# Costs of GpSimd's work in a list scheduler: wide operations in parts of 128 columns, four chunks converted early instead of five, four PSUM banks for y instead of five

## The chip, the cores and the metric

The kernel runs on one core of a Trainium2 chip. The metric is device time in microseconds of the whole program. Three runs of the kernel before took 821.39, 822.38 and 822.40 us (median 822.38 us). PE is the matrix engine TensorE, DVE is VectorE, ACT is ScalarE, POOL is GpSimd, SP issues the DMAs.

## What is computed

Three blocks follow each other, all in fp32:

```python
a = exp(phi - max(phi, axis=2)); a = a / (sum(a, axis=2) + 1e-9)
k_m, v_m = einsum('bhsm,bhsd->bhmd', a, k), einsum('bhsm,bhsd->bhmd', a, v)   # 32 memory slots
attn = softmax(q @ k_m^T / 8);  x = attn @ v_m          # 4 batches, 8 heads, 576 positions, 64 wide
h = x @ w_in;  g = maximum(0.01 * h, h);  x = g @ w_out                # 2304 x 512, inner width 2048
y = ((x @ w_a) * (x @ w_b)) @ w_out2                                   # inner width 1536
```

## The kernel before

Each fp32 product is made as three products of parts: a tensor is split into a high part (a rounded copy) and a low part (the tensor less its high part), and the products high*high, high*low and low*high are added in PSUM. So each operand needs a copy and a subtraction on ACT, DVE or POOL. The weights are first brought to another bit form: for each 512 KB tile of weights ACT makes two passes, and then `clamp` (L455), `shift` (L459), `join` (L463) and `add` (L466) follow, then the copy `hi` and the subtraction `lo` (L472). `shift` and `join` are DVE's alone; `clamp`, `add` and `lo` may go to DVE or to POOL.

The first MLP goes through four chunks c of 512 inner columns and, in each, eight tiles n of 288 tokens: four units h (24 matmuls in all), each followed by two passes of ACT and a subtraction g (L789, on DVE or POOL), and four units y (48 matmuls), each of which DVE adds into an accumulator (L815). Before the tiles of a chunk stand the products vw (L724), whose results ACT and DVE take from PSUM. The second MLP goes through twelve chunks of 128 columns, twice: for half s=0 and half s=1 of the tokens. Each chunk needs a tile of w_a, of w_b and of w_out2, and sums of w_a and w_b (`ws`, L954) with their splits (`wo`, L971). The first PRE chunks (5 before) are converted beside the first MLP and kept in HBM; the others are converted in half s=0 when they come, and kept too; half s=1 reads all of them back. PSUM's eight banks b0 to b7 are given to kinds of tiles by the table ROOMS: h has b0 to b2, y of the first chunk b3 and b4, y of the later chunks (`yx`) b3 to b7, vw and the other small products (`x`) b5 to b7.

The order of every engine's work is set by a list scheduler in the kernel itself (class `Program`) when the program is built. It knows a cost for each operation on each engine that may do it, gives each operation a latest time from its consumers, and goes forward in time: the free engine takes the most urgent ready operation, if no other engine would finish it sooner (`POOL_BIAS` of 0.8 us is counted against POOL) and a buffer is free. Operations of class `Port` on DVE and POOL exclude each other in its plan. It repeats this up to six times and keeps the shortest plan. On the chip each engine then works through its own list in order, and waits for semaphores where data or buffers come later than planned. The conversions are in these lists among the additions and subtractions that PE waits for.

The names that matter below: `c_pool2` (L69, POOL's cost of an operation with n columns), `two` (L362, an operation for DVE or POOL), `weight` (L429) with its costs, `y_unit` (L793, which takes its bank from `yx` from the second chunk on), `w_sums`, and PRE.

Of the kernel before, what the change touches and what calls it, by code (L numbers as in the profile page):

```python
# [66 lines left out]


def c_pool2(n):  # L69
    return 0.25 + n * 2.15e-3  # L70


def c_dve2(n):
# [14 lines left out]
class Op:  # L90
# [3 lines left out]
class Program:  # L94
# [58 lines left out]
    def order(self, target):  # L153
# [25 lines left out]
        ends, times, done, now, got = [], [0.0, 1.7], [], 0.0, {}  # L179
# [33 lines left out]
        main = sorted((o for o in self.ops if o.pos is not None), key=lambda o: o.pos)  # L213
        index = {o.seq: i for i, o in enumerate(main)}
        nth = 0
        while left:
# [59 lines left out]
            if times:  # L276
                nxt = min(nxt, times[0])
            if nxt > 5000:
                raise RuntimeError(f"no room: at {now} main {main[nth:nth+1] and main[nth].tiles} held {sorted(map(str,(k for k,t in held.items() if t[0]!='b')))}  ready {[(e, [x.tiles for x in r][:4]) for e, r in ready.items() if r]}")
            now = nxt  # L280
            while ends and ends[0][0] <= now + 1e-9:
                o = self.ops[heappop(ends)[1]]
# [6 lines left out]
    def run(self, make, rounds=6):  # L289
        main = [o for o in self.ops if o.pos is not None]  # L290
        main.sort(key=lambda o: o.pos)
        target, t = {}, START
        for o in main:
            target[o.seq] = t
            t += o.cost
        best, self.tries = None, []
        for _ in range(rounds):
            self.urgency(target)
            done, got = self.order(target)
            end = max(o.end for o in done)  # L300
# [23 lines left out]
def tile_mem_attention__leaky_mlp__bilinear_mlp(  # L324
# [20 lines left out]
    nc = tc.nc  # L345
# [8 lines left out]
    op, tile_of = pr.op, pr.tile  # L354
# [2 lines left out]
        pool = ps if tag[0] == "b" else sb  # L357
        return pool.tile([parts, *shape], dtype, tag=tag, name="_".join(map(str, key)))

    engines = {"DVE": nc.vector, "POOL": nc.gpsimd}  # L360

    def two(n):  # L362

# [30 lines left out]
    def zeros(T):  # L394
# [34 lines left out]
    def weight(kind, c, k, after=()):  # L429
# [44 lines left out]
        a = ("a", key)  # L474
# [1 line left out]
        op("DMA", c_dma(524288), load, r=after, w=[raw], tiles=[raw], ahead=1e12 if early else 30.0, keep=8 if early else 2 if late else 7 if c < 2 else 4)  # L476
        op("ACT", 0.66, high, r=[raw], w=[a], tiles=[raw, cv], ahead=1e12 if early else 25.0, keep=6 if early else 0 if late else 5 if c < 2 else 2)
        op("ACT", 0.66, low, r=[raw], w=[("l", key)], tiles=[raw, cv], ahead=any_time)
        op(Port({"DVE": 0.42, "POOL": 2.0}), 0, clamp, w=[a], tiles=[cv], ahead=any_time)
        op(Port({"DVE": 0.42}), 0, shift, w=[a], tiles=[cv], ahead=any_time)  # L480
        op(Port({"DVE": 0.68}), 0, join, r=[raw], w=[a], tiles=[raw, cv], ahead=any_time)
        op(Port({"DVE": 0.62, "POOL": 1.35}), 0, add, r=[("l", key)], w=[a], tiles=[cv], ahead=any_time)
        if kind in ("wa", "wb"):
            return
        if kind == "wout2" and by_seven(1, c):
# [866 lines left out]
```

## Time and profile before

| | |
|---|---|
| median of three runs | 822.38 us |
| profiled execution, whole | 821.03 us |
| its span, first to last instruction | 819.3 us |
| PE, DVE, ACT, POOL busy | 785.8, 681.0, 374.6, 239.2 us |
| PE's waits, longest in total | for ACT's first exponential 6.0 us, for DVE's kvn 4.1, for DVE's g 3.9, for DVE's accumulator 3.2 |
| first MLP / second MLP, about | 50 to 410 us / 410 to 819 us |

A busy PE is one that has matmuls in flight; with no wait 112 matmuls of 512 columns start in 25 us. What a wait on PE costs is read from stretches in which PE's busy time is under the stretch's length, and from the granted clock. What makes PE wait is read from the list of waits and from the rows of the engine named there, in order of time: the length of one instruction against the length that its form has when nothing is beside it.

### The profile page before, as it was taken

How to read it: one execution, taken by the hardware profiler on the slowest of the kernel's cores; microseconds unless marked ns; L12 is line 12 of the kernel's file. 1: busy time of each engine (PE TensorE's matmuls, PEld its weight loads, DVE VectorE, ACT ScalarE, POOL GpSimd, SP SyncE). 2: the span in 40 equal slices, each digit the busy share in tenths (PEclk: the TensorE clock that was granted, in tenths of full speed). 3: DMA queues.
4: the chain of work that ended last, by engine and by line, in shares of the span. 5: the costliest groups of instructions: out<-in, count | busy, mean ns of one | idle time of the engine just before them, and what ended most of it. 6: DMA issues, size and time to landing. Idle time of an engine off the chain costs nothing.

```text
span 819.3 us, 13254 instructions
## 1 busy us (share of the span) xinstructions
PE 785.8 (96%) x4898; PEld 700.9 (86%) x4898; DVE 681.0 (83%) x1225; ACT 374.6 (46%) x811; POOL 239.2 (29%) x223
## 2 busy tenths in 40 slices
PE   5789999999889999999999999999999999999998
PEld 4568899999889998999988888888888888887886
DVE  6998898689978999899674889999975686898875
ACT  5656776776546664665232534343411153122010
POOL 5562446124601352155000023332300131254300
PEclk8899999999989999999999999999999999999999
DMA  9885301074224530424797565574579788655402
GB/s 331 312 276 174 130 1 53 27 254 152 73 88 172 206 124 27 168 78 180 270 335 281 167 240 198 205 239 173 208 282 330 266 270 284 232 187 194 161 1 102
DMA packets 55936, 152.64 MB, mean 186 GB/s; under 512 B 6976, under 2 KB 20288, under 8 KB 55872
## 3 DMA queue, kind: packets, MB, share of 16 engines
q1 hardware_dynamic: 55872, 151.80, 53.4%
q8 instruction: 38, 0.62, 0.3%
q14 instruction: 26, 0.21, 0.1%
HBM read 106.17 MB, written 45.61 MB: 185 GB/s over the span
## 4 chain that ended last, share of the span: by engine, by line
PE 76%; DVE 14%; DMA 5%; issue 3%; ACT 1%; POOL 0%; SPq 0%; DVEq 0%; ACTq 0%
PE y L803 16%; PE o L1099 13%; PE aby L1016 11%; PE h L773 8%; PE abx L1016 7%; PE abz L1016 7%; PE os L1215 4%; DVE g L789 3%; PE b L1067 2%; PE a L1067 2%; PE vw L724 2%; DMA raw_wout<-in_w_out_dram 1%; DVE acc L815 1%; DVE cv_win L463 1%; DVE cv_win L455 1%
## 5 line engine op out<-in xcount | busy, mean ns | idle before, releaser
L803 PE MATMUL y<-g,wout 128*128 128x288 f32 x1536 | 224.1, 299 | 5.2 <-DVE g L789 3.9
L803 PEld LDWEIGHTS y<-g,wout 128*128 128x128 f32 x1536 | 212.8, 191 | 9.6 <-DVE g L789 4.6
L1016 PE MATMUL aby<-yb_T,wo 128*128 128x512 f32 x432 | 110.1, 390 | 0.8 <-DVE t L1024 0.8
L1016 PEld LDWEIGHTS aby<-yb_T,wo 128*128 128x128 f32 x432 | 80.1, 188 | 17.2 <-DVE t L1024 1.2
L1099 PE MATMUL o<-p,wout 128*128 128x512 f32 x384 | 94.2, 390 | 0.0
L1024 DVE TENSOR_TENSOR t<-aby,t 128x512 f32<-128x512 f32 x72 | 49.4, 686 | 48.3 <-PE aby L1016 46.4
L1099 PEld LDWEIGHTS o<-p,wout 128*128 128x128 f32 x384 | 71.9, 188 | 15.4 <-DVE osum L1112 0.3
L773 PE MATMUL h<-ahi,vwh 128*128 128x288 f32 x256 | 76.5, 299 | 1.2 <-ACT ahi L371 1.2
L773 PE MATMUL h<-alo,vwh 128*128 128x288 f32 x256 | 75.9, 297 | 0.8 <-POOL alo L672 0.8
L773 PE MATMUL h<-ahi,vwl 128*128 128x288 f32 x256 | 75.7, 296 | 0.0
L1016 PE MATMUL abx<-yb_B,wo 128*128 128x512 f32 x288 | 73.5, 391 | 0.4 <-ACT t L1027 0.4
L750 ACT ACTIVATE g<-h 128x288 fp32r<-128x288 f32 x128 | 52.5, 410 | 43.5 <-PE h L773 40.3
L789 DVE TENSOR_TENSOR g<-t,g 128x288 fp32r<-128x288 f32 x100 | 60.7, 611 | 5.8 <-ACT t L750 5.5
L1016 PEld LDWEIGHTS abx<-yb_B,wo 128*128 128x128 f32 x288 | 53.2, 188 | 11.3 <-ACT t L1027 0.8
L815 DVE TENSOR_TENSOR acc<-y,acc 128x288 f32<-128x288 f32 x96 | 43.0, 451 | 12.9 <-PE y L803 12.2
L750 ACT ACTIVATE t<-h 128x288 f32<-128x288 f32 x128 | 52.3, 408 | 0.0
L773 PEld LDWEIGHTS h<-ahi,vwh 128*128 128x128 f32 x256 | 48.2, 188 | 3.9 <-issue 2.4
L773 PEld LDWEIGHTS h<-alo,vwh 128*128 128x128 f32 x256 | 48.3, 189 | 1.3 <-POOL alo L672 1.2
L773 PEld LDWEIGHTS h<-ahi,vwl 128*128 128x128 f32 x256 | 48.3, 189 | 0.0
L739 DVE TENSOR_TENSOR vwl<-vw,vwh 64x512 fp32r<-64x512 f32 (+1 forms) x64 | 39.8, 621 | 7.0 <-ACT vwh L371 5.5
L371 ACT CAST p<-t 128x512 fp32r<-128x512 f32 x29 | 18.0, 619 | 55.8 <-DVE t L1045 29.0
L371 ACT CAST vwh<-vw 64x512 fp32r<-64x512 f32 (+2 forms) x61 | 30.6, 504 | 24.2 <-PE vw L724 17.5
(367 smaller groups left out, 1503.9 us busy)
## 6 DMA issues: line engine op xcount, KB each, us to landing
k_wo<-wo SPq DMA_DIRECT2D x28, 512.0 KB, 4.0
wo<-k_wo SPq DMA_DIRECT2D x28, 512.0 KB, 4.2
raw_wout<-in_w_out_dram SPq DMA_DIRECT2D x23, 512.0 KB, 5.4
raw_win<-in_w_in_dram SPq DMA_DIRECT2D x16, 512.0 KB, 6.4
kv<-in_kv_dram SPq DMA_DIRECT2D x16, 512.0 KB, 9.2
k_yb_T<-yb_T SPq DMA_DIRECT2D x8, 512.0 KB, 6.4
yb_T<-k_yb_T SPq DMA_DIRECT2D x8, 512.0 KB, 5.0
raw_wa<-in_w_a_dram SPq DMA_DIRECT2D x7, 512.0 KB, 4.6
```

The source lines that it names most:

```text
L371: nc.scalar.copy(dst, src)
L739: nc.vector.tensor_tensor(T[lk][to, j // 2, cols], T[o][i * 64:(i + 1) * 64, :], T[hk][to, j // 2, cols].bitcast(F32), op=ALU.subtract)
L750: nc.scalar.activation(dst, src, AF.Prelu, alpha=0.01)
L773: nc.tensor.matmul(T[o], T[w[u]][:, k, fs], T[a[v]][:, k, cols], start=(k == 0 and i == 0), stop=(k == 1 and i == 2))
L789: lambda T, e: engines[e].tensor_tensor(T[g][:, i, 1, :], T[t], T[g][:, i, 0, :].bitcast(F32), op=ALU.subtract),
L803: nc.tensor.matmul(T[o], w[:, u, es], g[:, v, :], start=(f == 0 and i == 0), stop=(f == 3 and i == 2))
L815: "DVE", c_dve(NB), lambda T: nc.vector.tensor_tensor(T[acc][:, e, :], T[o], T[acc][:, e, :], op=ALU.add),
L1016: nc.tensor.matmul(T[o], T[w][:, which, u, k * P:(k + 1) * P], T[ys[v]][:, k, :], start=first and k == 0 and x == 0, stop=k == 1 and x == ...
L1024: op("DVE", 0.69, lambda T: nc.vector.tensor_tensor(T[to], T[o], T[x], op=ALU.add), r=[o, x], w=[to], tiles=[o, x, to])
L1067: nc.tensor.matmul(T[o], T[w][:, k // 2, u, k % 2 * P:(k % 2 + 1) * P], T[ys[v]][:, k, :], start=(k == 0 and x == 0), stop=(k == 3 and x = ...
L1099: nc.tensor.matmul(T[o], T[w][:, u, es], T[g][:, at, v, :], start=(x == 0 and k == 0), stop=(x == 1 and k == 2))
L1215: nc.tensor.matmul(T[o], lhs(T, u), T[g][:, v, :], start=k == 0, stop=k == 2)
```

## The change

POOL's costs in the scheduler are new, and the operations of 448 columns or more that POOL gets are issued as four instructions of 128 columns each (or 64 times 2). PRE is 4, and `yx` has four banks, so that b7 is left to `x`. If a round of the scheduler finds no room, the best plan so far is taken.

```diff
-    "yx": ["b3", "b4", "b5", "b6", "b7"],
+    "yx": ["b3", "b4", "b5", "b6"],
...
-PRE = 5
+PRE = 4
...
 def c_pool2(n):
-    return 0.25 + n * 2.15e-3
+    return 0.45 + n * 1.5e-3 if n < 448 else n * 4.8e-3
...
+            try:
+                done, got = self.order(target)
+            except NoRoom:
+                if best is None:
+                    raise
+                break
...
-    engines = {"DVE": nc.vector, "POOL": nc.gpsimd}
+    class InParts:
+        @staticmethod
+        def cuts(ap):
...
+            if size < 448:
+                return [(slice(None),)]
+            m = size // shape[-1]
+            k = max(1, 128 // m) if shape[-1] * m > 128 else shape[-1]
+            return [(slice(None),) * len(shape) + (slice(i, min(shape[-1], i + k)),) for i in range(0, shape[-1], k)]
+
+        def tensor_tensor(self, dst, a, b, op):
+            for x in self.cuts(dst):
+                nc.gpsimd.tensor_tensor(dst[x], a[x], b[x], op=op)
...
+    engines = {"DVE": nc.vector, "POOL": InParts()}
...
-        op(Port({"DVE": 0.42, "POOL": 2.0}), 0, clamp, w=[a], tiles=[cv], ahead=any_time)
+        op(Port({"DVE": 0.42, "POOL": 2.45}), 0, clamp, w=[a], tiles=[cv], ahead=any_time)
...
-        op(Port({"DVE": 0.62, "POOL": 1.35}), 0, add, r=[("l", key)], w=[a], tiles=[cv], ahead=any_time)
+        op(Port({"DVE": 0.62, "POOL": 2.45}), 0, add, r=[("l", key)], w=[a], tiles=[cv], ahead=any_time)
```

A price of 2.45 us in place of 1.35 us moves work from POOL's list to DVE's: POOL has 100 operations of 448 columns or more before and 51 after (in parts), DVE 1225 instructions before and 1273 after. PE's instructions are the same ones, in a slightly other order. SP issues five reads of kept tiles fewer, in half s=0, and as many loads and writes as before. Three places in the lists follow. Names carry the chunk, the tile and a running number; `x4` is four instructions that follow each other.

POOL in the first chunk of the first MLP, from the first two subtractions alo to the last g of tile 0, before:

```order
L672 TENSOR_TENSOR alo_0_418<-at_0_1_0_408,ahi_0_411 128x288
L466 TENSOR_TENSOR cv_wout_0_0_306<-cv_wout_0_0_306 128x512
L789 TENSOR_TENSOR g_0_0_0_451<-t_0_0_0_457,g_0_0_0_451 128x288
L472 TENSOR_TENSOR wout_0_0_461<-cv_wout_0_0_306,wout_0_0_461 128x512
L472 TENSOR_TENSOR wout_0_1_504<-cv_wout_0_1_330,wout_0_1_504 128x512
L789 TENSOR_TENSOR g_0_0_0_451<-t_0_0_1_478,g_0_0_0_451 128x288
L472 TENSOR_TENSOR wout_0_3_540<-cv_wout_0_3_393,wout_0_3_540 128x512
L789 TENSOR_TENSOR g_0_0_1_509<-t_0_0_2_512,g_0_0_1_509 128x288
L789 TENSOR_TENSOR g_0_0_1_509<-t_0_0_3_573,g_0_0_1_509 128x288
```

and with the change:

```order
L387 TENSOR_TENSOR alo_0_424<-at_0_1_0_414,ahi_0_417 128x288
L387 TENSOR_TENSOR g_0_0_0_456<-t_0_0_0_462,g_0_0_0_456 128x288
L387 TENSOR_TENSOR g_0_0_0_456<-t_0_0_1_472,g_0_0_0_456 128x288
L387 TENSOR_TENSOR wout_0_0_483<-cv_wout_0_0_309,wout_0_0_483 128x128 x4
L387 TENSOR_TENSOR g_0_0_1_510<-t_0_0_2_518,g_0_0_1_510 128x288
L387 TENSOR_TENSOR wout_0_3_550<-cv_wout_0_3_399,wout_0_3_550 128x128 x4
L387 TENSOR_TENSOR g_0_0_1_510<-t_0_0_3_577,g_0_0_1_510 128x288
```

The add of wout_0_0 and the subtraction of wout_0_1 have gone to DVE, where the add stands ahead of the instructions kvn that PE waits for and the subtraction behind them; the two g of the first pair come ahead of the wide work.

POOL in the second chunk of the first MLP (c=1), from tile n=3 to the last of the wide operations before the third chunk, before:

```order
L472 TENSOR_TENSOR wout2_0_-1_2625<-cv_wout2_0_-1_2197,wout2_0_-1_2625 128x512
L472 TENSOR_TENSOR win_2_0_2642<-cv_win_2_0_2465,win_2_0_2642 128x512
L466 TENSOR_TENSOR cv_wb_1_-1_2480<-cv_wb_1_-1_2480 128x512
L466 TENSOR_TENSOR cv_wout_2_0_2756<-cv_wout_2_0_2756 128x512
L954 TENSOR_TENSOR ws_1_2859<-cv_wb_1_-1_2480 128x256
L954 TENSOR_TENSOR ws_1_2859<-cv_wa_1_-1_2414,cv_wb_1_-1_2480 128x256
L954 TENSOR_TENSOR ws_1_2859<-ws_1_2859,cv_wa_1_-1_2414 128x256
L472 TENSOR_TENSOR wout_2_0_2886<-cv_wout_2_0_2756,wout_2_0_2886 128x512
L466 TENSOR_TENSOR cv_wout_2_2_2824<-cv_wout_2_2_2824 128x512
L954 TENSOR_TENSOR ws_1_2859<-cv_wa_1_-1_2414,ws_1_2859 128x256
L971 TENSOR_TENSOR wo_-1_1_2_2913<-ws_1_2859,wo_-1_1_2_2913 128x2x256
L971 TENSOR_TENSOR wo_-1_1_1_2895<-cv_wb_1_-1_2480,wo_-1_1_1_2895 128x2x256
```

and with the change:

```order
L391 TENSOR_SCALAR cv_wb_1_-1_2516<-cv_wb_1_-1_2516 128x128 x4
L387 TENSOR_TENSOR wout2_0_-1_2643<-cv_wout2_0_-1_2233,wout2_0_-1_2643 128x128 x4
L387 TENSOR_TENSOR cv_wa_1_-1_2450<-cv_wa_1_-1_2450 128x128 x4
L387 TENSOR_TENSOR g_1_7_1_3011<-t_1_7_3_3047,g_1_7_1_3011 128x288
L387 TENSOR_TENSOR wout_2_3_3042<-cv_wout_2_3_2921,wout_2_3_3042 128x128 x4
L387 TENSOR_TENSOR ws_1_3195<-cv_wa_1_-1_2450,ws_1_3195 128x256
```

Twelve operations have become six, and chunk 1 of the second MLP is converted later: its sums and splits, which stood here, come in the third chunk. From tile n=3 to the first tiles of the third chunk DVE has 105 instructions before and 103 with the change.

POOL in half s=0 of the second MLP, chunks 8 to 10, before:

```order
L971 TENSOR_TENSOR wo_0_9_0_6555<-cv_wa_9_0_6414,wo_0_9_0_6555 128x2x256
L954 TENSOR_TENSOR ws_9_6603<-cv_wa_9_0_6414,cv_wb_9_0_6435 128x256
L971 TENSOR_TENSOR wo_0_9_1_6611<-cv_wb_9_0_6435,wo_0_9_1_6611 128x2x256
L954 TENSOR_TENSOR ws_9_6603<-ws_9_6603,cv_wa_9_0_6414 128x256
L954 TENSOR_TENSOR ws_9_6603<-cv_wa_9_0_6414,ws_9_6603 128x256
L971 TENSOR_TENSOR wo_0_9_2_6665<-ws_9_6603,wo_0_9_2_6665 128x2x256
L971 TENSOR_TENSOR wo_0_9_3_6675<-ws_9_6603,wo_0_9_3_6675 128x2x256
L466 TENSOR_TENSOR cv_wa_10_0_6646<-cv_wa_10_0_6646 128x512
L971 TENSOR_TENSOR wo_0_10_0_6827<-cv_wa_10_0_6646,wo_0_10_0_6827 128x2x256
L455 TENSOR_SCALAR cv_wb_11_0_6837<-cv_wb_11_0_6837 128x512
L466 TENSOR_TENSOR cv_wb_11_0_6837<-cv_wb_11_0_6837 128x512
```

and with the change:

```order
L391 TENSOR_SCALAR cv_wa_10_0_6721<-cv_wa_10_0_6721 128x128 x4
L391 TENSOR_SCALAR cv_wb_10_0_6746<-cv_wb_10_0_6746 128x128 x4
L387 TENSOR_TENSOR ws_9_6821<-cv_wb_9_0_6511 128x256
L387 TENSOR_TENSOR ws_9_6821<-cv_wa_9_0_6487,cv_wb_9_0_6511 128x256
L387 TENSOR_TENSOR ws_9_6821<-cv_wa_9_0_6487,ws_9_6821 128x256
L387 TENSOR_TENSOR wo_0_9_1_6811<-cv_wb_9_0_6511,wo_0_9_1_6811 128x2x64 x4
L387 TENSOR_TENSOR p_0_8_0_6905<-t1_0_8_6724,p_0_8_0_6905 128x128 x4
L391 TENSOR_SCALAR cv_wa_11_0_6918<-cv_wa_11_0_6918 128x128 x4
L391 TENSOR_SCALAR cv_wb_11_0_6951<-cv_wb_11_0_6951 128x128 x4
L391 TENSOR_SCALAR cv_wout2_10_0_6998<-cv_wout2_10_0_6998 128x128 x4
L391 TENSOR_SCALAR cv_wout2_11_0_7020<-cv_wout2_11_0_7020 128x128 x4
```

POOL's splits have gone to DVE and DVE's clamps have come to POOL. In chunks 8 to 10 DVE has 93 instructions before and 99 with the change; POOL has 8 wide and 4 narrow operations before, 11 wide (9 of them clamps) and 5 narrow ones with the change.

## Rows read from the trace of the kernel before

**Rows 1.** The page's first part: busy time of the engines, share of the span, instructions.

```profile
PE 785.8 (96%) x4898; PEld 700.9 (86%) x4898; DVE 681.0 (83%) x1225; ACT 374.6 (46%) x811; POOL 239.2 (29%) x223
```

**Rows 2.** Busy time of each engine in stretches: start and end in us, length, then PE, PEld, DVE, ACT, POOL with their instructions, granted clock of PE, DMA share, GB/s.

```profile
25.00:50.00 25.00, 17.46 (x152) 12.21 (x151) 23.69 (x51) 14.88 (x40) 15.48 (x19) 0.84 0.86 284
...
200.00:225.00 25.00, 23.07 (x170) 22.37 (x168) 25.00 (x41) 14.91 (x35) 13.20 (x11) 1.00 0.29 103
225.00:250.00 25.00, 21.98 (x136) 21.08 (x137) 19.37 (x37) 12.66 (x30) 2.25 (x2) 0.86 0.39 129
...
274.00:315.00 41.00, 39.43 (x294) 39.12 (x294) 40.84 (x71) 23.23 (x55) 17.34 (x12) 1.00 0.30 99
...
423.00:457.00 34.00, 34.00 (x174) 29.09 (x173) 14.87 (x26) 10.85 (x20) 0.00 (x0) 1.00 0.80 291
...
553.00:612.00 59.00, 59.00 (x306) 50.72 (x306) 53.32 (x93) 20.60 (x37) 12.91 (x11) 1.00 0.60 218
612.00:629.00 17.00, 17.00 (x98) 14.96 (x98) 8.82 (x16) 2.50 (x5) 0.00 (x0) 1.00 0.97 348
...
750.00:775.00 25.00, 23.69 (x105) 19.31 (x104) 23.50 (x36) 3.37 (x6) 11.23 (x6) 1.00 0.54 182
```

**Rows 3.** The same view, stretches of the second chunk of the first MLP and what follows.

```profile
184.00:228.00 44.00, 39.25 (x287) 38.08 (x285) 44.00 (x70) 25.24 (x58) 23.30 (x18) 1.00 0.33 117
...
228.00:232.00 4.00, 3.26 (x12) 2.73 (x11) 3.81 (x8) 2.48 (x5) 0.00 (x0) 0.53 0.32 131
232.00:236.00 4.00, 4.00 (x21) 3.96 (x20) 2.51 (x5) 1.00 (x2) 1.92 (x1) 0.62 0.00 0
```

**Rows 4.** PE's waits: who waited, for whom, us in total, times, longest.

```profile
PE kvt L570 <- DVE kvn L562: 4.1, 2, 3.9
PE y L803 <- DVE g L789: 3.9, 3, 1.8
PE vw L724 <- DVE acc L815: 3.2, 2, 2.4
...
PE os L1215 <- DVE osum L1240: 1.3, 1, 1.3
...
PE y L803 <- ACT acc L371: 0.9, 1, 0.9
```

**Rows 5.** DVE in order of time from 217 us: start, length, engine, line, operation, tiles, count.

```profile
217.35 1.42 DVE L789 TENSOR_TENSOR g<-t,g 128x288 fp32r<-128x288 f32 x1
218.70 1.22 DVE L463 SCALAR_TENSOR_TENSOR cv_wout<-raw_wout,cv_wout 128x512 int32<-128x512 int32 x1
219.83 0.45 DVE L815 TENSOR_TENSOR acc<-y,acc 128x288 f32<-128x288 f32 x1
220.20 3.12 DVE L466 CUSTOM_DVE_ANT_0 cv_wout<-cv_wout 128x1024 uint16<-128x1024 uint16 x2
223.25 0.45 DVE L789 TENSOR_TENSOR g<-t,g 128x288 fp32r<-128x288 f32 x1
```

**Rows 6.** POOL in the same stretch.

```profile
217.20 1.26 POOL L466 TENSOR_TENSOR cv_wout<-cv_wout 128x512 int32<-128x512 int32 x1 [1.99 <-issue]
218.42 0.94 POOL L954 TENSOR_TENSOR ws<-cv_wa_-1_2414,ws 128x256 f32<-128x256 f32 x1
219.33 1.74 POOL L971 TENSOR_TENSOR wo_-1_1_2_2913<-ws,wo_-1_1_2_2913 128x512 fp32r<-128x512 f32 x1
221.03 1.74 POOL L971 TENSOR_TENSOR wo_-1_1_1_2895<-cv_wb_-1_2480,wo_-1_1_1_2895 128x512 fp32r<-128x512 f32 x1
```

**Rows 7.** Groups of DVE's instructions by line and shape: count, busy us, mean ns of one, idle before.

```profile
L463 DVE SCALAR_TENSOR_TENSOR cv_wa<-raw_wa,cv_wa 128x512 int32<-128x512 int32 x7 | 4.8, 684 | 0.0
L466 DVE CUSTOM_DVE_ANT_0 cv_wb<-cv_wb 128x1024 uint16<-128x1024 uint16 x6 | 4.1, 685 | 0.1
```

**Rows 8.** Groups of POOL's instructions by line and shape, the same columns.

```profile
L455 POOL TENSOR_SCALAR cv_wout<-cv_wout 128x512 f32<-128x512 f32 x4 | 8.4, 2103 | 3.2 <-ACT cv_wout L448 3.1
L971 POOL TENSOR_TENSOR wo<-cv_wb,wo 128x512 fp32r<-128x512 f32 x6 | 7.8, 1293 | 3.1 <-ACT wo L371 3.1
...
L789 POOL TENSOR_TENSOR g<-t,g 128x288 fp32r<-128x288 f32 x28 | 25.2, 904 | 42.7 <-ACT t L750 31.2 <-PE h L773 11.3
...
L954 POOL TENSOR_TENSOR ws<-cv_wb 128x256 f32<-128x256 f32 x2 | 1.5, 740 | 6.3 <-PE aby L1016 6.2
```

**Rows 9.** DVE and POOL in order of time at three other places: DVE's subtractions with an operand in PSUM beside two wide operations of POOL, and DVE's alo beside a clamp on POOL.

```profile
142.89 4.22 DVE L739 TENSOR_TENSOR vwl<-vw,vwh 64x512 fp32r<-64x512 f32 x6 [0.52 <-ACT vwh L371]
...
144.36 2.54 POOL L472 TENSOR_TENSOR wout<-cv_wout,wout 128x512 fp32r<-128x512 f32 x2 [0.72 <-ACT wout L371]
...
119.47 0.88 DVE L672 TENSOR_TENSOR alo<-at,ahi 128x288 fp32r<-128x288 f32 x2
...
118.56 1.98 POOL L455 TENSOR_SCALAR cv_wout<-cv_wout 128x512 f32<-128x512 f32 x1
```

**Rows 10.** DVE ahead of PE's longest wait for it in the first 50 us, in order of time.

```profile
34.02 4.16 DVE L463 SCALAR_TENSOR_TENSOR cv_wout<-raw_wout,cv_wout 128x512 int32<-128x512 int32 x4
38.11 1.76 DVE L466 CUSTOM_DVE_ANT_0 cv_wout<-cv_wout 128x1024 uint16<-128x1024 uint16 x1
...
40.56 2.34 DVE L466 CUSTOM_DVE_ANT_0 cv_wout<-cv_wout 128x1024 uint16<-128x1024 uint16 x2
...
44.05 2.13 DVE L656 TENSOR_TENSOR sm<-sm,mx 128x288 f32<-128x288 f32 x2
```

More of the change, by code (lines that the diff above doesn't have):

```diff
@@ L85 @@
 class Port(dict):
+    pass
+class NoRoom(RuntimeError):
     pass
@@ L278, in order @@
             if nxt > 5000:
-                raise RuntimeError(f"no room: at {now} main {main[nth:nth+1] and main[nth].tiles} held {sorted(map(str,(k for k,t in held.items() if t[0]!='b')))}  ready {[(e, [x.tiles for x in r][:4]) for e, r in ready.items() if r]}")
+                raise NoRoom(f"no room: at {now} main {main[nth:nth+1] and main[nth].tiles} held {sorted(map(str,(k for k,t in held.items() if t[0]!='b')))}  ready {[(e, [x.tiles for x in r][:4]) for e, r in ready.items() if r]}")
             now = nxt
@@ L298, in run @@
             self.urgency(target)
-            done, got = self.order(target)
+            try:
[4 more added lines that the diff above has]
+                break
             end = max(o.end for o in done)
@@ L358, in make, with tensor_scalar @@
         return pool.tile([parts, *shape], dtype, tag=tag, name="_".join(map(str, key)))
-    engines = {"DVE": nc.vector, "POOL": nc.gpsimd}
+    class InParts:
+        @staticmethod
+        def cuts(ap):
+            shape = tuple(ap.shape[1:])
+            size = 1
+            for n in shape:
+                size *= n
+            if size < 448:
[6 more added lines that the diff above has]
+                nc.gpsimd.tensor_tensor(dst[x], a[x], b[x], op=op)
+        def tensor_scalar(self, dst, a, *scalars, **ops):
+            for x in self.cuts(dst):
+                nc.gpsimd.tensor_scalar(dst[x], a[x], *scalars, **ops)
+    engines = {"DVE": nc.vector, "POOL": InParts()}
     def two(n):
```

## The prediction

> **What bounds the kernel now.** I read the busy times first: PE is busy for 96% of the span, DVE for 83%, POOL for 29% [rows 1]. Behind a PE so full, only what makes PE wait can be won, so the list of PE's waits came next. Behind the start DVE is named in nearly all of them: kvn 4.1 us, g 3.9, the accumulator's addition 3.2, osum 1.3 [rows 4]. The stretches say where these are. From 200 to 250 us PE is busy for 45.05 us of 50, and its clock shows 0.86 in the second half; from 274 to 315 us it lacks 1.57 us of 41; from 750 to 775 us it lacks 1.31 [rows 2]. In half s=0 of the second MLP, 553 to 612 us, it lacks nothing, though DVE is busy for 53.32 us of 59 [rows 2].
>
> In the worst place, 184 to 228 us, DVE is busy for all 44.00 us and PE for 39.25 [rows 3]: DVE sets the pace. Behind it PE runs at 0.53 and 0.62 of its clock for 4 us each [rows 3]. At the half level (1.2 of 2.4 GHz) this loses 4 x 0.47 + 4 x 0.38 = 3.4 us, after PE had waited.
>
> Why DVE is full there is seen in order of time. A subtraction g takes 0.45 us when nothing is beside it (at 223.25), and took 1.42 at 217.35; a join took 1.22 in place of 0.68 and two adds 3.12 in place of 1.37 [rows 5, 7]. Beside them four operations ran on POOL, 5.68 us in sum [rows 6]. DVE lost 0.97 + 0.54 + 1.75 = 3.26 us, 0.58 us for each us of POOL. The addition with an operand in PSUM took its 0.45 [rows 5], and six subtractions from PSUM 4.22 us, 0.70 each, beside wide POOL work [rows 9]. So POOL delays DVE's instructions that take all from SBUF. For the whole stretch this gives 23.30 x 0.58 = 13.5 us of DVE's 44.
>
> **The change part by part.** *Price of a part.* No row shows 128 columns on POOL. A subtraction takes 1.29 us for 512 columns and 0.74 for 256 [rows 8], so 2.2 ns a column and 0.19 us each; my estimate is 0.46 for 128, 1.85 for four. A clamp takes 2.10 for 512 [rows 8]; with the same 0.19 us at the start four parts are about 2.7. The bounds are the whole operation (1.29; 2.10) below and four times the 256-column row (2.96) above. I take the estimates, which lie between neighbours of the same form. DVE does the same subtraction in 0.68 us alone; as an operation of 1.3 us on POOL costs it up to 1.3 x 0.58 = 0.75, sending it to DVE costs DVE nothing where DVE is full. So DVE's 48 more instructions are no loss by themselves; what counts is which work stands where.
>
> *Stretch 184 to 228 us.* The order has six operations on POOL for twelve, and 103 DVE instructions for 105 up to the third chunk. The six are a clamp, three wide subtractions or adds in parts, a g (0.90) and a sum (0.74): 2.7 + 5.6 + 1.6 = 9.9 us, and I take 11 for what stands before them. DVE then needs 44.0 - 13.5 + 11 x 0.58 = 36.9 us, under PE's 39.25. So 4.75 us of PE's wait go, with them the 0.74 at 228 to 232 and the 3.4 of the clock: 8.9 us at most [rows 3]. Next behind DVE stand ACT's copies of vw, for which no wait of PE is listed. I take 7.5; bounds 0 (POOL's parts hold DVE as before) and 8.9.
>
> *Stretch 274 to 315 us.* POOL has 17.34 us [rows 2]; with the change four wide operations (two splits, an add and a later subtraction) and five narrow ones, about 7.4 + 4 = 11.4. DVE gets three instructions more (1.8 us): 40.84 - (17.34 - 11.4) x 0.58 + 1.8 = 39.2, about PE's 39.43. I take -1.5 with bounds 0 and -2.
>
> *Start.* PE waits 3.9 us for kvn. Ahead of it four joins took 4.16, three adds 1.76 and 2.34, two subtractions 2.13 [rows 10]. With the change POOL has two wide operations in parts there for four whole ones, and DVE one add more (0.6). POOL's time falls from 4 x 1.6 to 3.7 us, at 0.58 that is 1.6 for DVE, less 0.6: 1.0. Not all of it reaches PE, whose other inputs come late too: -0.5, bounds +1 and -2.
>
> *The fifth chunk.* Its three tiles cost DVE or POOL 12 steps, four sums and five splits, 21 instructions at DVE's 53.32 / 93 = 0.57 us [rows 2], 12 us. They leave the first MLP, which is what thins the stretches above, and come to half s=0. From 423 to 457 us DVE is busy for only 14.87 of 34 us and POOL for none [rows 2]: room for all of it. But the later chunks slide too: chunks 8 to 10 have 99 DVE instructions for 93, + 6 x 0.6 = 3.7 us, and POOL 9 clamps, 2 other wide operations and 5 narrow ones: 24.3 + 3.7 + 4 = 32 us for 12.91. What a clamp does to DVE decides. Beside one, two alo took 0.88 us, their undisturbed length [rows 9]. With clamps at nothing and the rest at 0.58, DVE needs 53.32 + 3.7 + (7.7 - 12.91) x 0.58 = 54.0 of 59; with all at 0.58 it needs 68.1, 9 us too much, of which the 8 idle us behind (612 to 629 [rows 2]) return little to PE. I take +2, by the row; bounds 0 and +9. The reads saved cost PE nothing before, since PE lacks nothing there.
>
> *Four banks for y.* Waits for a bank of y sum to 0.9 + at most 3.2 us [rows 4]. With one bank fewer, y may lag DVE by one unit less (12 matmuls, some 1.6 us); with b7 kept free, vw no longer waits for the accumulator. The two are counted as 0, bounds -1 and +3. The last wait, 750 to 775 us, keeps its instructions within one: 0, bounds -1.3 and +1.
>
> The sum: -7.5 - 1.5 - 0.5 + 2 = -7.5. Against the profiled execution's 821.03 us (span 819.3 and 1.7 around it) that is 813.5; the median of the runs lies 1.35 us higher: 814.9, and I say 815.
>
> A rule against this sum: the Trainium skill's page "SBUF — State Buffer", section "Who interferes with whom", has DVE and GpSimd share a pair of SBUF ports under an exclusive lock: the one that issues first keeps it for its whole instruction, and the other blocks. It agrees with the delayed g and the undelayed PSUM rows above, but not with the two alo beside the clamp. By this rule all POOL time in parts would be lost to a DVE that always wants the ports, and the time would be that of the first rival.
>
> **The rivals.** *The parts hold DVE off fully.* Four parts give POOL four turns, and after each DVE instruction a part is already waiting; DVE then loses all of POOL's time, 1.0 in place of 0.58. In 184 to 228 us DVE needs 44 - 13.5 + 11 = 41.5, more than PE's 39.25, and of 8.9 us only about 3 are won; nothing from 274 to 315; in chunks 8 to 10 DVE needs 53.32 + 3.7 + 32 - 7.5 = 81.5 for 59, of which the idle 8 behind take a part: +12 or more. Together 822.4 - 3 + 12 = 831; it decides from about 0.7 us lost per us of POOL. For it: the clamps wait in one block, with DVE's shifts and joins behind each. Against it: the alo row, and the instructions on PSUM, which run on.
>
> *The waits only move.* PE waits less for g, but the conversions now come later, closer to their use, and PE waits for those, about as long: half of 8.9 is won and the same lost in chunks 8 to 11: 822. For it: in chunk 8's time chunk 9 is being converted, where before it was chunk 10. Against it: no wait of PE for a converted weight is listed now.
>
> *All of it.* If chunks 8 to 10 cost nothing and both first-MLP stretches give all, with 2 us at the start: 822.4 - 8.9 - 2 - 2 = 809.5, and 806 with vw's and osum's waits gone.
>
> **How the numbers follow.** The forecast (809 to 820) has 0.5, all of it 0.09, a smaller gain 0.01, the moved waits 0.14, the full hold 0.26. Below 0.2% (1.6 us) this kernel's measurement cannot tell from no change. Nearly all of the first three is faster, 0.6; the moved waits give same 0.13 and slower 0.01, with the full hold 0.27. The forecast alone reaches 809 to 820; the range takes in most of the first rival's lighter outcomes, 806 to 827.
>
> **What would show it.** Right: the four-part instructions near 0.46 us (clamps 0.6 to 0.7); PE full from 184 to 236 us at clock 1.00; DVE below 40 us of 44 there; no PE wait for DVE of over 1 us in chunks 7 to 11. Wrong: g still at over 1 us beside parts; PE waiting in half s=0 for wo or for DVE's additions; a new half-clock stretch behind 50 us; y waiting for DVE's accumulator for want of the fifth bank.

## The result and the profile after

The kernel after takes 808.16 us (median of four runs, 807.13 to 809.07) against 821.88 us for the kernel before on the same chip: a ratio of 0.9835, 95% interval 0.9815 to 0.9856. The profiled execution took 809.07 us, its span is 807.3. In the page's first part PE's work is what it was [rows 1]; DVE has 48 instructions more and is busy 13 us less, POOL is busy 24 us less:

```profile
PE 784.9 (97%) x4898; PEld 700.0 (87%) x4898; DVE 667.7 (83%) x1273; ACT 375.8 (47%) x817; POOL 215.2 (27%) x328
```

The stretches of [rows 2, 3], and one that is new (650 to 675 us). The columns are those of [rows 2]:

```profile
25.00:50.00 25.00, 19.65 (x162) 14.71 (x161) 23.79 (x56) 15.76 (x43) 16.16 (x28) 0.77 0.78 265
184.00:228.00 44.00, 44.00 (x325) 43.53 (x324) 40.03 (x80) 26.27 (x60) 12.90 (x18) 1.00 0.32 104
228.00:232.00 4.00, 4.00 (x31) 3.92 (x30) 3.84 (x9) 1.16 (x2) 0.00 (x0) 1.00 0.00 0
232.00:236.00 4.00, 4.00 (x33) 4.00 (x32) 3.90 (x9) 3.12 (x9) 0.82 (x1) 1.00 0.02 6
...
274.00:315.00 41.00, 40.96 (x299) 40.21 (x299) 37.72 (x76) 21.48 (x49) 8.02 (x12) 1.00 0.35 116
423.00:457.00 34.00, 34.00 (x185) 29.57 (x184) 27.63 (x51) 20.17 (x38) 4.31 (x6) 1.00 0.68 250
553.00:612.00 59.00, 59.00 (x325) 51.46 (x324) 49.80 (x88) 19.27 (x37) 23.73 (x34) 1.00 0.74 249
...
650.00:675.00 25.00, 22.82 (x99) 18.15 (x98) 13.47 (x23) 11.88 (x21) 0.74 (x1) 1.00 0.77 253
...
750.00:775.00 25.00, 25.00 (x112) 20.69 (x111) 21.83 (x35) 3.67 (x6) 5.26 (x8) 1.00 0.29 97
```

These are the same times, not the same work: from 236 us to the end the kernel after is 9 to 14 us ahead in its work. From 184 to 236 us PE is full, at clock 1.00, and DVE has 4 us left of the first 44. In the list of PE's waits those for g, for the accumulator and for DVE's osum [rows 4] are gone. The waits for km and kvn lie in the first 50 us. What is left behind them is small, but one entry is new, os waiting for ACT's osum:

```profile
PE km L586 <- DMA kvr<-in_kv_rest_dram: 2.5, 1, 2.5
PE kvt L603 <- DVE kvn L595: 2.4, 1, 2.4
...
PE os L1248 <- ACT osum L404: 2.2, 2, 1.5
...
PE aby L1049 <- DVE t L1057: 0.5, 1, 0.5
```

To see where the 12.0 us between the two profiled spans lie, I counted PE's work in both traces: every matmul at the median distance to the next of its form (0.227 us for 512 columns, 0.132 for 288, 0.120 for 256), and compared the times at which the same amount was done; by this count the two are 11.8 us apart at the end. The table gives the gaps between these times; "before" says at what time of the kernel before the stretch ends.

| up to (before) | after against before, running | this stretch | place |
|---|---|---|---|
| 155.8 us | -0.3 | -0.3 | start, first chunk of the first MLP |
| 196.0 us | -0.4 | 0 | |
| 245.7 us | -9.6 | -9.2 | the worst place of before, and its half clock |
| 306.2 us | -9.6 | 0 | |
| 328.8 us | -11.8 | -2.2 | |
| 389.2 us | -11.7 | 0 | |
| 431.2 us | -13.4 | -1.7 | change to the second MLP |
| 651.3 us | -13.5 | 0 | all of half s=0 |
| 731.7 us | -10.2 | +3.3 | the new waits |
| 773.2 us | -11.8 | -1.6 | near the end |

The new wait, in order of time on DVE, ACT and PE from 658.5 us (start, length, engine, line, operation, tiles):

```profile
658.52 0.76 DVE L1177 TENSOR_TENSOR w2s<-wf 128x256 f32<-128x256 f32 x2 [2.42 <-DMA wf<-k_wf]
...
659.69 0.62 ACT L404 CAST w<-w2s 128x512 fp32r<-128x512 f32 x1 [2.97 <-DVE w2s L1177]
660.22 0.58 ACT L404 COPY osum<-os 128x512 f32<-128x512 f32 x1
660.85 0.96 PE L1248 MATMUL os<-pb_T,w 128*128 128x512 f32 x3 [0.68 <-ACT osum L404]
...
662.83 0.62 ACT L404 CAST w<-w2s 128x512 fp32r<-128x512 f32 x1 [2.03 <-DMA k_wout<-wout]
...
664.06 1.08 ACT L404 COPY osum<-os 128x512 f32<-128x512 f32 x2
664.70 0.98 PE L1248 MATMUL os<-pb_B,wout 128*128 128x512 f32 x3 [1.50 <-ACT osum L404]
```

ACT stands in its list at a copy of w. The sums it copies wait for a tile wf that lands late, and the next copy for a buffer that a store still reads. The osum that frees PE's bank is behind these copies of w. ACT is busy for 11.88 us of these 25: what blocks is the order, not its load.

### The profile page after: what moved, and what is told of

Same layout as the page of the kernel before. It is cut to its first block, busy times and chain, and to the rows that moved or that the text cites. A ratio compares the mean times of both kernels' runs of the same rounds, so it can differ in the third digit from the quotient of the medians.

```text
span 807.3 us, 13391 instructions
## 1 busy us (share of the span) xinstructions
PE 784.9 (97%) x4898; PEld 700.0 (87%) x4898; DVE 667.7 (83%) x1273; ACT 375.8 (47%) x817; POOL 215.2 (27%) x328
## 4 chain that ended last, share of the span: by engine, by line
PE 93%; DMA 3%; DVE 2%; issue 1%; ACT 0%; SPq 0%; DVEq 0%; ACTq 0%
PE y L836 26%; PE o L1132 13%; PE h L806 12%; PE aby L1049 12%; PE abz L1049 8%; PE abx L1049 8%; PE os L1248 4%; PE vw L757 2%; PE b L1100 2%; PE a L1100 2%; PE sc L674 1%; DMA kvr<-in_kv_rest_dram 1%; DMA k_wout<-wout 1%; PE km L586 1%; DMA raw_win<-in_w_in_dram 1%
## 5 line engine op out<-in xcount | busy, mean ns | idle before, releaser
L836 PE MATMUL y<-g,wout 128*128 128x288 f32 x1536 | 221.0, 297 | 0.0
L822 DVE TENSOR_TENSOR g<-t,g 128x288 fp32r<-128x288 f32 x102 | 49.0, 484 | 4.5 <-ACT t L783 4.4
L387 POOL TENSOR_TENSOR g<-t,g 128x288 fp32r<-128x288 f32 x26 | 26.4, 1017 | 76.0 <-ACT t L783 58.6
```

The source lines that it names most:

```text
L822: lambda T, e: engines[e].tensor_tensor(T[g][:, i, 1, :], T[t], T[g][:, i, 0, :].bitcast(F32), op=ALU.subtract),
L836: nc.tensor.matmul(T[o], w[:, u, es], g[:, v, :], start=(f == 0 and i == 0), stop=(f == 3 and i == 2))
```

## The experiments

The change has four parts, which the plan binds together: the parts of 128 columns, the prices, PRE and the banks. The open questions were which of them frees DVE, and what a part costs it. "Prices" below are the planned cost of one wide operation on POOL; the prices of the narrow ones that POOL gets (256 and 288 columns) differ by less than 0.04 us between the old list and the new. All ratios are to the kernel before on the same chip.

**Whole operations on the lists of after.**

```diff
-    engines = {"DVE": nc.vector, "POOL": InParts()}
+    engines = {"DVE": nc.vector, "POOL": nc.gpsimd}
```

> The lists of the kernel after, word for word, but every operation on POOL is one instruction again (51 of 448 columns or more). Theory 'plan' (the new prices and the shorter early conversion keep wide work off POOL, so DVE has room): nothing hangs on the grain. 51 whole operations of 1.3 to 2.1 us cost POOL less time than four parts of 0.67 us each, and DVE some 51 x (0.64 - 0.36) = 14 us of delay more, of which most falls where DVE has room: 807 to 812 us against 808 for the kernel after. Theory 'parts' (the fine grain is what frees DVE): the waits for DVE between 184 and 315 us come back, and its delay rises from 27 to over 55 us: 815 to 822 us.

813.27 us, ratio 0.9883 (0.9862 to 0.9903): between the two. By the profile's page, with the same 1273 instructions, DVE is busy 11.4 us longer than with parts, and POOL 52 us shorter. POOL has 53 operations of 448 columns or more here, as in the kernel after: the 51 that are named have 512 columns, and two have 448. DVE's loss is 0.22 us for each:

```profile
PE 783.1 (97%) x4898; PEld 698.7 (86%) x4898; DVE 679.1 (84%) x1273; ACT 375.2 (46%) x817; POOL 163.0 (20%) x169
```

The worst place of before stays nearly clean without parts:

```profile
184.00:228.00 44.00, 43.41 (x319) 42.82 (x319) 40.74 (x80) 25.99 (x59) 7.25 (x5) 1.00 0.30 103
```

So the lists empty that place, and the parts are worth 5 us elsewhere. In the count of PE's work this profiled execution is 3.3 us behind that of the kernel after, and 2.6 of them come between 732 and 773 us (times of the kernel before). There DVE's subtraction pb_T and addition osum, 0.68 us each alone, stand beside wide operations of POOL, and PE's os waits for DVE:

```profile
738.70 3.44 POOL L1212 TENSOR_TENSOR pb_B<-pf,pb_B 128x512 fp32r<-128x512 f32 x2
...
740.92 1.77 DVE L1212 TENSOR_TENSOR pb_T<-pT,pb_T 128x512 fp32r<-128x512 f32 x1
742.62 1.77 DVE L1265 TENSOR_TENSOR osum<-osum,osum 128x512 f32<-128x512 f32 x1
...
745.04 0.96 PE L1248 MATMUL os<-pb_T,w 128*128 128x512 f32 x3 [1.50 <-DVE osum L1273]
```

What the parts change is seen in one pair of instructions. The same subtraction on POOL stands beside the same one on DVE (0.68 us alone, the median of its form with nothing on POOL); whole, in this run:

```profile
220.94 1.29 POOL L505 TENSOR_TENSOR wout<-cv_wout,wout 128x512 fp32r<-128x512 f32 x1
221.05 1.72 DVE L505 TENSOR_TENSOR wout<-cv_wout,wout 128x512 fp32r<-128x512 f32 x1
```

and in parts, in the kernel after:

```profile
221.28 2.18 POOL L387 TENSOR_TENSOR wout<-cv_wout,wout 128x128 fp32r<-128x128 f32 x4
221.39 0.90 DVE L505 TENSOR_TENSOR wout<-cv_wout,wout 128x512 fp32r<-128x512 f32 x1
```

DVE loses 1.04 us to the whole operation and 0.22 to the four parts, and POOL takes 0.89 longer. About 0.55 of this is the price of four instructions for one (four parts of 0.46 us, the length with little beside them that is shown further below, against 1.29); the rest is POOL's waiting.

**Parts on the lists of before.**

```diff
-    engines = {"DVE": nc.vector, "POOL": nc.gpsimd}
+    engines = {"DVE": nc.vector, "POOL": InParts()}
```

> The lists of the kernel before, word for word, but the 100 wide operations on POOL are each four instructions of 128 columns. Theory 'parts': DVE's delay beside POOL falls from 73 to about 45 us, and PE's waits for DVE between 184 and 236 us go: 812 to 816 us. Theory 'plan': the lists are what counts; four parts take 2.67 us where the plan has 1.35, so POOL is late by over 1 us per operation, and what waits for POOL takes the place of what waited for DVE: 820 to 830 us. The rival 'parts hold DVE off fully' of the prediction would give over 830.

822.95 us, ratio 1.0001 (0.9983 to 1.0019). DVE is busy 21.4 us less than before for the same 1225 instructions, POOL 85 us more, and the time is the same:

```profile
PE 789.5 (96%) x4898; PEld 703.1 (85%) x4898; DVE 659.6 (80%) x1225; ACT 373.6 (45%) x811; POOL 323.8 (39%) x523
```

Why is in PE's waits and, in order of time, in POOL near 380 us: a split of the fifth chunk and two other wide operations stand ahead of the g that PE wants. The wait costs 4.6 us in the count of PE's work. It is not the only loss of this profiled execution, the slowest of its twelve: a longer wait for ACT's copy of y costs 2.4 us between 100 and 156 us, and the first 75 us cost 2.2, with a wait of 3.6 us for a load. Against them 2.3 us are won from 196 to 246 us, 0.9 from 306 to 329 and 1.4 near the end. What was won in one place was lost in another. Theory 'plan' held.

```profile
PE y L836 <- POOL g L387: 4.6, 2, 2.8
...
PE y L836 <- ACT acc L404: 2.2, 1, 2.2
```

```profile
375.72 2.16 POOL L387 TENSOR_TENSOR wo_-1_4_2_4985<-ws,wo_-1_4_2_4985 128x128 fp32r<-128x128 f32 x4
...
377.84 2.87 POOL L387 TENSOR_TENSOR yt_T<-acc,yt_T 128x128 f32<-128x128 f32 x4
...
380.68 3.91 POOL L387 TENSOR_TENSOR yb_B<-acc,yb_B 128x128 fp32r<-128x128 f32 x4
...
384.56 1.23 POOL L387 TENSOR_TENSOR yl<-acc,yl 128x256 fp32r<-128x256 f32 x1
...
385.75 1.00 POOL L387 TENSOR_TENSOR g<-t,g 128x288 fp32r<-128x288 f32 x1
```

**Four early chunks on the kernel before**, and nothing else.

```diff
-PRE = 5
+PRE = 4
```

> The kernel before with one thing changed: four chunks are converted beside the first MLP in place of five. Old prices, whole operations on POOL (101 of them), five banks for y. The runs with parts at the old prices took 823.0 us with five early chunks and 818.3 with four (and four banks). Theory 'fifth chunk' (its 21 conversions, some 12 us of DVE's work, weigh in the first MLP with whole operations too): 815 to 818.5 us. Theory 'it pays only with parts' (the 4.7 us came of POOL's late parts, of which there were fewer): 820.5 to 823 us, as before.

822.8 us, ratio 1.0013 (0.9999 to 1.0028): the second expectation held. The worst place is what it was [rows 3]:

```profile
184.00:228.00 44.00, 39.25 (x285) 37.84 (x283) 44.00 (x71) 25.05 (x58) 23.21 (x17) 1.00 0.33 116
```

**The old prices in the kernel after**, with four banks for y, and then with five.

```diff
-    return 0.45 + n * 1.5e-3 if n < 448 else n * 4.8e-3
+    return 0.25 + n * 2.15e-3
...
-        op(Port({"DVE": 0.42, "POOL": 2.45}), 0, clamp, w=[a], tiles=[cv], ahead=any_time)
+        op(Port({"DVE": 0.42, "POOL": 2.0}), 0, clamp, w=[a], tiles=[cv], ahead=any_time)
...
-        op(Port({"DVE": 0.62, "POOL": 2.45}), 0, add, r=[("l", key)], w=[a], tiles=[cv], ahead=any_time)
+        op(Port({"DVE": 0.62, "POOL": 1.35}), 0, add, r=[("l", key)], w=[a], tiles=[cv], ahead=any_time)
```

> The kernel after with the old price list: four early chunks, four banks and parts stay, but POOL is planned 101 wide operations at 1.35 to 2 us where in parts they take 2.7 to 2.9. Theory 'plan': POOL comes late, the additions and subtractions behind the wide work come late, PE waits: 815 to 828 us. Theory 'parts': DVE is free at any price, 807 to 811 us. Theory 'fifth chunk' (the early chunk that left the first MLP is the whole gain): 807 to 811 too, and the run with four chunks alone would then tell it from 'parts'.

> Parts and four early chunks at the old prices, with five banks for y: the kernel before with the parts and the fifth chunk's move, and nothing else. No instruction changes its place against the run with four banks (818.3 us). At the old prices the parts alone left the time at 823.0 and the four chunks alone at 822.8. Theory 'the parts make POOL late, and the fifth chunk's leaving relieves POOL' (the 4.75 us at 383 us, where y waited for a g on POOL, are gone in the run at 818.3): 817 to 819.5 us. Theory 'banks' (with b7 free the additions' lateness no longer holds up vw): 821 to 824 us.

818.27 us (0.9944, 0.9926 to 0.9963) and 817.49 us (0.9933, 0.9911 to 0.9955): theory 'plan' held in the first, and in the second the theory that the parts make POOL late. So with parts the prices are worth 8 to 10 us (809.87 against 817.49 with five banks, 808.16 against 818.27 with four). With whole operations they are worth about the same: 813.27 against 822.8, both with four early chunks. The banks are worth nothing that can be told. With four early chunks the parts give 5 us at the new prices and at the old ones; with five and the old prices they gave none. No run has the new prices with five early chunks, so what PRE is worth there stays open. The trace with four banks shows POOL busy for 37.00 us of 44, where it was 23.30 before, and PE still short of full:

```profile
184.00:228.00 44.00, 42.60 (x314) 41.79 (x312) 41.47 (x73) 28.18 (x64) 37.00 (x52) 1.00 0.28 102
225.00:250.00 25.00, 21.58 (x142) 20.73 (x141) 20.39 (x39) 13.10 (x30) 10.22 (x17) 0.93 0.46 155
```

With b7 left to it, vw waits all the same, for an addition that comes late:

```profile
PE vw L757 <- DVE acc L848: 4.4, 2, 3.4
```

**Five banks for y in the kernel after.**

```diff
-    "yx": ["b3", "b4", "b5", "b6"],
+    "yx": ["b3", "b4", "b5", "b6", "b7"],
```

> The kernel after with the fifth bank, b7, given back to y. No instruction changes its place in any list; only the banks of y are handed out over five in place of four. Theory 'banks' (b7 kept free for vw is worth the 3.2 us for which vw waited for the accumulator before): vw waits again at the starts of the later chunks, 809.5 to 812 us. Theory 'no banks' (vw waited because DVE's additions were late, and they are not late now): 807 to 809 us, as the kernel after.

809.87 us, ratio 0.9842 (0.982 to 0.9864), which cannot be told from after. The time lies in the range of 'banks', but its trace has no wait of vw for the accumulator, and the stretch from 196 to 246 us gives the same 9.2 us. By the trace 'no banks' holds.

**The price alone, varied**: 1.9, 3.07 and 4.0 us for 512 columns (4.8e-3 becomes 3.7e-3, 6.0e-3 and 7.8e-3; the clamp's price becomes 2.2, 3.05 and 4.0, the add's 1.9, 3.05 and 4.0).

```diff
-    return 0.45 + n * 1.5e-3 if n < 448 else n * 4.8e-3
+    return 0.45 + n * 1.5e-3 if n < 448 else n * 3.7e-3
```

> The kernel after with a price for a wide operation on POOL of 1.9 us (clamp 2.2) in place of 2.46; POOL then has 71 of them in place of 51 (with the old price, 96). Theory 'true price' (the plan is good where the price is what the operation takes, 2.7 us): the time lies between that of the old prices and that of the kernel after, 810 to 816 us, with PE's waits for vw and g partly there. Theory 'any dearer price will do' (a threshold, passed at once): 807 to 809 us.

> The kernel after with a price of 3.07 us for a wide operation on POOL (clamp and add 3.05): POOL has 34 of them. Theory 'true price' (2.7 us is what they take): DVE gets 17 operations more than it should, 10 us of work for some 9 us less of POOL; slightly worse than after, 808 to 813 us. Theory 'less on POOL' (what counts is only that wide work leaves POOL, since DVE loses time beside it and PE waits for what stands behind it): better still, 803 to 807 us.

> As the run before, with a price of 4.0 us: POOL has 12 wide operations. Theory 'true price': DVE takes over 39 operations at 0.4 to 0.7 us, 24 us of its own time, for about 14 us of delay that goes, and is full again in the first MLP: 812 to 820 us. Theory 'less on POOL': 800 to 806 us.

| price, us | 1.35 | 1.9 | 2.46 | 3.07 | 4.0 |
|---|---|---|---|---|---|
| operations of 512 columns on POOL | 96 | 71 | 51 | 34 | 12 |
| median, us | 818.27 | 809.30 | 808.16 | 810.02 | 819.27 |
| DVE busy, us | 663.4 | 664.0 | 667.7 | 670.5 | 672.7 |
| POOL busy, us | 320.1 | 261.9 | 215.2 | 169.6 | 121.5 |

A flat floor from 1.9 to 3.07 us (the intervals overlap: 0.9833 to 0.9881, 0.9815 to 0.9856, 0.9837 to 0.9889) and some 10 us at either side. 'True price' held at 3.07, and 'less on POOL' fell. At 1.9 the time lies between the two ranges, and the flat floor hides two differences: the worst place gives 5.8 us there and not 9.2, since vw waits for late additions again (1.2 us), but the loss of 3.3 us at 660 us does not come. Each price is one plan, so small steps between them say little. At 4.0 I was right in the size and wrong in the place: DVE isn't full in the first MLP, where it has 6.6 us left of 44. Against the kernel after, 2.5 us are lost at the start (where runs differ by 2 us anyway), 2.9 at the change to the second MLP and 2.8 in half s=0, where PE waits for DVE and for ACT behind DVE:

```profile
184.00:228.00 44.00, 44.00 (x327) 43.64 (x326) 37.40 (x80) 26.87 (x61) 2.38 (x4) 1.00 0.24 79
400.00:425.00 25.00, 22.67 (x121) 19.07 (x121) 18.71 (x31) 8.54 (x14) 1.17 (x1) 1.00 0.82 294
575.00:600.00 25.00, 23.94 (x118) 19.74 (x117) 20.64 (x37) 7.47 (x14) 8.06 (x10) 1.00 0.60 212
```

**The grain**: parts of 256 and of 64 columns on the lists of after.

```diff
-            k = max(1, 128 // m) if shape[-1] * m > 128 else shape[-1]
+            k = max(1, 256 // m) if shape[-1] * m > 256 else shape[-1]
```

> The lists of the kernel after, the 51 wide operations on POOL as two instructions of 256 columns each in place of four of 128. Narrow operations of 256 columns cost DVE 0.15 to 0.29 us each in the traces so far, four parts of 128 0.36 and one whole 0.6. If DVE's delay follows the number of times it is caught (one per instruction on POOL, shorter with a shorter instruction), two parts lie between: 0.3 to 0.5 us per wide operation, about 33 us of delay in all, and 809 to 812 us. If the fine grain itself is what matters (128 columns are short enough to slip between DVE's instructions and 256 are not), this run stands with the whole operations: 812 to 814 us.

> The lists of the kernel after, the 51 wide operations on POOL as eight instructions of 64 columns each. DVE's delay per wide operation was 0.6 us whole, 0.5 in two parts and 0.36 in four. If it goes on falling with the grain: 0.2 to 0.3 us, and 806 to 809 us, unless POOL's own time decides. POOL's time per wide operation was 1.5, 1.9 and 2.67 us; a part of 128 columns had 0.45 at the least, so eight parts take at least 8 x 0.3 = 2.4 and, if each waits a turn behind DVE (0.2 us each, as a part of 128 does), 4 us. Then POOL's clamps and g come late and PE waits for POOL or for what stands behind it: 810 to 814 us.

810.23 us (0.9871, 0.9845 to 0.9897) and 808.67 us (0.9843, 0.9821 to 0.9865), both where a delay that falls with the grain put them. One group of POOL's instructions, the six subtractions of wout (count, busy us, mean ns), first whole, then in two, four and eight parts:

```profile
L505 POOL TENSOR_TENSOR wout<-cv_wout,wout 128x512 fp32r<-128x512 f32 x6 | 8.8, 1468 | 31.2 <-ACT wout L404 31.2
```

```profile
L387 POOL TENSOR_TENSOR wout<-cv_wout,wout 128x256 fp32r<-128x256 f32 x12 | 11.8, 1005 | 29.6 <-ACT wout L404 29.6
```

```profile
L387 POOL TENSOR_TENSOR wout<-cv_wout,wout 128x128 fp32r<-128x128 f32 x24 | 16.3, 711 | 28.2 <-ACT wout L404 28.2
```

```profile
L387 POOL TENSOR_TENSOR wout<-cv_wout,wout 128x64 fp32r<-128x64 f32 x48 | 19.8, 447 | 25.1 <-ACT wout L404 25.1
```

One operation keeps POOL busy for 1.47, 1.97, 2.72 and 3.30 us. For DVE, whose instructions are the same in all four, the pages have 679.1, 673.7, 667.7 and 667.3 us busy. So two parts give half of the gain in DVE's time, four give all of it, and eight only cost POOL more, for which PE waits 1.2 us at one g. Of the times, whole can be told from 128, and just from 64 (the intervals touch); 256 cannot be told from whole, from 128 or from 64.

**The new wait at 660 us**: the loads of wf get 4 us more of slack.

```diff
-        op("DMA", c_dma(524288), lambda T: nc.sync.dma_start(T[wf], kept(wf)), r=[("keptf", 2 * q), ("keptf", 2 * q + 1)], w=[wf], tiles=[wf], ahead=30.0, keep=2)
+        op("DMA", c_dma(524288), lambda T: nc.sync.dma_start(T[wf], kept(wf)), r=[("keptf", 2 * q), ("keptf", 2 * q + 1)], w=[wf], tiles=[wf], ahead=30.0, keep=2, slack=4.0)
```

> The kernel after with 4 us more of slack on one kind of load: the read of the kept w_out2 tiles for half s=1, for whose sums ACT waits at 658 to 663 us while PE waits for ACT's copies behind them (3.1 us lost between 650 and 675 us, 1.1 between 700 and 725). The loads are issued three to five places earlier; up to there the lists are those of the kernel after. Theory 'late load' (the new waits at 660 us are ACT's, blocked behind the sums of a tile that lands late): 804 to 806 us, the two losses gone. Rival (the queue is full there, and what is moved back, reads and stores of w_a's and w_b's parts, comes late in its turn): 807 to 810 us, with PE waiting for wo or for ACT elsewhere between 640 and 700 us.

804.3 us, ratio 0.9791 (0.9767 to 0.9815), the best of all. The load for these sums is issued at 639.86 us in place of 652.22, and both stretches are full:

```profile
650.00:675.00 25.00, 25.00 (x112) 20.72 (x111) 16.00 (x25) 11.79 (x21) 2.28 (x5) 1.00 0.81 256
700.00:725.00 25.00, 25.00 (x112) 20.71 (x111) 22.71 (x36) 6.19 (x10) 9.99 (x15) 1.00 0.68 228
```

'Late load' holds, for both losses. Behind this load the plan differs in other places too (DVE has 1269 instructions, not 1273), and what share of the loss the buffer had that a store still read is not separated.

## Why the prediction came out as it did

The direction was right, and so was the mechanism: DVE, delayed by POOL, held PE in the first MLP. The time, 808.16 us for a forecast of 815, lies below the forecast's own 809 to 820, where I had put the "all of it" case with a chance of 0.09. That it lies no lower is luck: the new loss at 660 us was not foreseen, and with it gone the time is 804.3, below the range. By the count of PE's work the terms compare so:

- *Stretch 184 to 236 us*, -7.5: all of it went, -9.2, the upper bound of 8.9 and a little more. For the work that PE did from 184 to 228 us before, DVE was busy for 35.20 us (I had 36.9) and POOL for 11.94 (I took 11), and PE waits for nothing:

```profile
183.60:222.10 38.50, 38.50 (x287) 38.30 (x286) 35.20 (x72) 24.15 (x56) 11.94 (x17) 1.00 0.29 96
```

- *Stretch 274 to 315 us*, -1.5 with -2 at most: -2.2, all that was lost there.
- *Start*, -0.5: -0.3 by 156 us. PE's wait for kvn fell from 3.9 to 2.4 us, and one for a load rose from 0.6 to 2.5. Between runs whose lists are the same up to there, the start differs by about 2 us, so this term isn't tested.
- *Fifth chunk and chunks 8 to 10*, +2 with 0 to +9: 0. This is the term that was mis-sized most. Its working was right. The work that PE did from 553 to 612 us before lies 13.5 us earlier in the kernel after, and there DVE is busy for 54.60 us of 59 (I had 54.0) beside 32.05 us of POOL (I had 32):

```profile
539.50:598.50 59.00, 59.00 (x307) 50.72 (x306) 54.60 (x96) 20.80 (x39) 32.05 (x45) 1.00 0.59 199
```

  The step that failed came behind it: DVE at 54.0 of 59 should leave PE full, as 53.32 had done before and 54.60 did now, and I still added 2 us that no row gave. The clamps at nothing were right too: four parts of one take 2.82 us, and the split and the difference beside them keep their length:

```profile
568.21 2.82 POOL L391 TENSOR_SCALAR cv_wout<-cv_wout 128x128 f32<-128x128 f32 x4 [0.56 <-ACT cv_wout L481]
569.24 0.69 DVE L1004 TENSOR_TENSOR wo<-cv_wa,wo 128x512 fp32r<-128x512 f32 x1 [1.15 <-ACT wo L404]
...
570.28 0.68 DVE L1057 TENSOR_TENSOR t<-abz,t 128x512 f32<-128x512 f32 x1
```

- *Four banks*, 0: right, by two pairs of runs.
- *End*, 0 with -1.3 at most: -1.6, all that was lost there [rows 2] and a little more. It is the parts that give it: with whole operations on the same lists there is a loss of 1.0 in its place.
- Not in the sum: -1.7 at the change to the second MLP, which comes with PRE alone too (-1.7 in that run), and +3.3 at 651 to 732 us. With the gain at the end they add to nothing, which is luck.

*Price of a part.* 0.46 us was forecast; the 142 parts of subtractions and adds took 0.66 on average, the 68 of clamps 0.73 for 0.67. The estimate is what a part takes where little stands beside it, as in this group of POOL's; the rest is POOL's waiting. Four parts, 2.65 us by their mean length, are near the scheduler's new 2.46.

```profile
L387 POOL TENSOR_TENSOR wo_-1_3_1_4535<-cv_wb_-1_4385,wo_-1_3_1_4535 128x128 fp32r<-128x128 f32 x4 | 1.7, 460 | 0.0
```

*DVE loses 0.58 us for each us of POOL.* That was one stretch with whole operations, and for them it was right: in all of 184 to 228 us before, DVE's delays sum to 14 us (I had 13.5). For parts it was not: over the same work after, they sum to 2.2 us, where I had 11 x 0.58 = 6.4. Over the whole trace I took each DVE instruction's time beyond the median of its form with nothing on POOL: 73.5 us before, 26.7 after. Per us of POOL the wide operations cost 0.35 before (54.9 us of 157) and their parts 0.11 (15.6 of 144). The error changed little in the sum, since DVE came out under PE's time by the 0.58 as well.

*That the fifth chunk's leaving "thins the stretches above"* was wrong: with PRE alone nothing changes at 184 to 228 us. The prices thin them.

The first rival, that parts hold DVE off fully, fell: it needed 0.7 us lost per us of POOL, and 0.11 were. The rule of the Trainium skill's page "SBUF — State Buffer", section "Who interferes with whom", by which the later of the two blocks until the earlier is through, agrees with the pair at 221 us as far as one instruction goes (1.04 us lost beside a whole operation of 1.29). My step from it, that a part would always be waiting ahead of DVE, did not hold: POOL's parts wait too, 0.71 us each in the group of wout against 0.46 with little beside them. The second rival, that the waits move, fell in its size (it took back the whole gain) and its place. One wait did move: PE waits for ACT, which waits for a load, and not for a converted weight.

Of the signs that I named, PE's full stretch, its clock, and the missing waits in chunks 7 to 11 came. DVE stood at 40.03 us against "below 40", which is at the line, and the parts were longer.

## What to carry to other kernels

Where a planner has two engines that disturb each other, the price of the disturbing one decides more than its grain: here 8 to 10 us for the price and 5 for the parts, and the parts alone gave nothing, since a queue that becomes slower than its plan makes new waits. A price near what the operation takes in company did best here (it takes 2.65 us; 1.9 to 3.07 did, 1.35 and 4.0 did not). After a gain, read the list of waits again: a load whose slack was enough for the slower kernel cost 3.3 us, and 4 us more of slack on it brought them back.

## What the runs showed of the hardware

- An operation on POOL in four parts keeps POOL busy nearly twice as long as in one piece (2.72 us for 1.47) and delays DVE far less; the gain for DVE ends at parts of 128 columns (667.7 us busy, and 667.3 with 64).
- What one instruction of DVE lost beside a single instruction of POOL went up to a value that follows POOL's columns: about 1.1 us beside a subtraction or add of 512 columns, 0.55 beside 256, 0.27 beside 128 and 0.13 beside 64. Most lost nothing.
- A clamp on POOL, which reads one tensor, costs DVE less even whole: 0.22 us for one of 2.0 us, and 0.04 for a part, by the count of delays, against 0.59 and 0.09 for a subtraction. The most that one instruction lost beside it was 0.42 us whole and 0.10 for a part.
- In the middle of the kernel before, PE's granted clock fell to its lower level once, behind the stretch in which PE had waited 4.75 us [rows 3]; with those waits gone it shows 1.00 in every stretch from 75 to 800 us. Not every wait brings it down: from 650 to 675 us PE lacks 2.18 us of 25, at 1.00.
